# Decode attention on one core: keys and values streamed together in sets of four groups, with the softmax maximum

## The chip, the core and the metric

The kernel runs on one core of a Trainium2 chip. The metric is the device time of one execution in microseconds; the lower the better. A core has five engines that run side by side: PE (matrix multiply, with its weight loads shown as PEld), DVE (vector), ACT (activations), POOL and SP. Each works through its own list of instructions in order and waits on semaphores for the others. SP, ACT and POOL also issue transfers, which 16 DMA engines carry out.

## What is computed

The reference normalises x (8 rows of 512), and runs two branches on it: attention against cached keys and values, and a gated feed-forward network. Cut to what matters:

```python
xn = _layernorm(x)
q = (xn @ wq)                     # 8 rows, 32 heads of 128
k = k_cache[:, :, Sk - W:, :]     # W = 1024 of 4096 positions, 8 kv heads, 4 query heads each
v = v_cache[:, :, Sk - W:, :]
scores = einsum("bhqd,bhkd->bhqk", q, k) * 128 ** -0.5
p = softmax(scores)
s = einsum("bhqk,bhkd->bhqd", p, v) ... @ wo
g = silu((gelu(xn @ w_gate) * (xn @ w_up)) @ w_down)
return x + s * g
```

A pair of a kv head and a batch row is called a group here: 64 groups, each with 1,024 keys and 1,024 values of 128 bf16 numbers (256 KB each) and four query rows.

## The kernel before

It is written in tiles; a scheduler orders the instructions of each engine from their dependencies and allocates buffers, so the program's order is only a hint.

**Weights.** SP issues x (L74) and wq (L77, 4 MB in one transfer); ACT issues w_gate and w_down (L79, L83), POOL issues w_up (L81). The three queues share the 16 DMA engines.

**Head.** x is normalised (L90 to L99), transposed (L120), and multiplied by wq in 128 small products (L135) into q, kept transposed as `qT_all`. The feed-forward branch is two up-projections (L153), an activation chain between ACT and DVE (L163 to L177), the down-projection of 14 products with 512 columns (L181) and the gate `g_sb` (L189 to L193).

**Key stage.** For each group: a 256 KB load of keys (L203, six buffers), eight 128x128 transposes on PE into one PSUM bank (L211), a copy of the 1,024 columns to SBUF on DVE (L217), eight products of the transposed keys with the four query columns (L221), and an Exp on ACT (L228), without subtracting a maximum, into `pT_all`, which holds all 64 groups.

**Sums.** Four products with a matrix of ones, 512 columns each (L243), each reduced on DVE (L252), and one reciprocal of 256 columns (L258).

**Value stage.** For each group: a 256 KB load of values (L269, 20 buffers), eight products of four columns (L277) and a multiplication by the reciprocal (L284). After each kv head, 512 KB of wo are loaded (L292) and four products of 512 columns add that head's projection to `s_ps` (L300).

**End.** Two DVE instructions (L309, L311) and the store (L312).

Of the kernel before, what the change touches and what calls it, by code (L numbers as in the profile page):

```python
# [12 lines left out]
FP32 = mybir.dt.float32  # L13


@with_exitstack
def kernel(
# [12 lines left out]
):  # L30
    nc = tc.nc

# [7 lines left out]
    NDC = D // 128  # L40
    NFC = F // 128
    NSC = W // 128
    inv_sqrt_dh = float(Dh) ** -0.5

    P = nc.NUM_PARTITIONS
    NG = Hkv * B
    GB = 16
# [6 lines left out]
    kT_pool = ctx.enter_context(tc.tile_pool(name="kT_pool", bufs=4))  # L54
    v_pool = ctx.enter_context(tc.tile_pool(name="v_pool", bufs=20))
    small = ctx.enter_context(tc.tile_pool(name="small", bufs=3))
# [11 lines left out]
    )  # L68
    ones_pp = consts.tile([P, P], BF16, name="ones_pp")
    nc.vector.memset(ones_pp, 1.0)  # L70

    x_flat = A_x.flatten_outer_dims()
    x_sb = persist.tile([B, D], BF16, name="x_sb")
    nc.sync.dma_start(out=x_sb, in_=x_flat)  # L74

    wq_sb = weights.tile([P, NDC, Hq * Dh], BF16, name="wq_sb")
    nc.sync.dma_start(out=wq_sb, in_=A_wq.rearrange("(k p) n -> p k n", p=P))  # L77
    wg_sb = weights.tile([P, NDC, F], BF16, name="wg_sb")
    nc.scalar.dma_start(out=wg_sb, in_=B_w_gate.rearrange("(k p) n -> p k n", p=P))  # L79
    wu_sb = weights.tile([P, NDC, F], BF16, name="wu_sb")  # L80
    nc.gpsimd.dma_start(out=wu_sb, in_=B_w_up.rearrange("(k p) n -> p k n", p=P))  # L81
    wd_sb = weights.tile([P, NFC, D], BF16, name="wd_sb")
    nc.scalar.dma_start(out=wd_sb, in_=B_w_down.rearrange("(k p) n -> p k n", p=P))  # L83
    wo_sb = weights.tile([P, Hq, D], BF16, name="wo_sb")

    eps_sb = consts.tile([B, 1], FP32, name="eps_sb")
    nc.vector.memset(eps_sb, 1e-5)

# [17 lines left out]
    )  # L106

    xnT_sb = persist.tile([P, NDC, B], BF16, name="xnT_sb")
    qT_all = persist.tile([P, B, Hq], BF16, name="qT_all")
    oT_all = persist.tile([P, Hq, B], BF16, name="oT_all")  # L110
    hT_sb = persist.tile([P, NFC, B], BF16, name="hT_sb")
    g_sb = persist.tile([B, D], FP32, name="g_sb")
    pT_all = persist.tile([P, NG, NSC, rep], BF16, name="pT_all")
    sums_sb = persist.tile([P, NG, rep], FP32, name="sums_sb")
    recip_all = persist.tile([P, NG, rep], FP32, name="recip_all")

    with tc.tile_pool(name="ps_xnT", bufs=1, space=bass.MemoryType.PSUM) as ps_xnT_pool:
        xnT_ps = ps_xnT_pool.tile([P, NDC, B], BF16, name="xnT_ps")
        for k in range(NDC):
            nc.tensor.transpose(  # L120
                xnT_ps[:, k, :],
                xhat[:, k * 128 : (k + 1) * 128],
                ident[0:B, 0:B],
            )
        nc.vector.tensor_copy(out=xnT_sb, in_=xnT_ps)

    HB = 8
    qctx = ExitStack()
    ps_q = qctx.enter_context(tc.tile_pool(name="ps_q", bufs=2, space=bass.MemoryType.PSUM))
    for m0 in range(0, Hq, HB):  # L130
        qT_ps = ps_q.tile([P, HB, B], FP32, name="qT_ps")
        for mi in range(HB):
            m = m0 + mi
            for k in range(NDC):
                nc.tensor.matmul(  # L135
                    qT_ps[:, mi, :],
                    wq_sb[:, k, m * Dh : (m + 1) * Dh],
                    xnT_sb[:, k, :],
                    start=(k == 0),
                    stop=(k == NDC - 1),  # L140
                )
        nc.vector.tensor_copy(  # L142
            out=qT_all[:, :, m0 : m0 + HB],
            in_=qT_ps.rearrange("p h b -> p b h"),
        )

    fctx = ExitStack()
    ffn_ps = fctx.enter_context(tc.tile_pool(name="ffn_ps", bufs=1, space=bass.MemoryType.PSUM))
    gu_ps = ffn_ps.tile([P, NFC, 2, B], FP32, name="gu_ps")
    for j in range(NFC):  # L150
        for w, wsb in enumerate((wg_sb, wu_sb)):
            for k in range(NDC):
                nc.tensor.matmul(  # L153
                    gu_ps[:, j, w, :],
                    wsb[:, k, j * 128 : (j + 1) * 128],
                    xnT_sb[:, k, :],
                    start=(k == 0),
                    stop=(k == NDC - 1),
                )
    zT = gu_ps[:, :, 0, :]  # L160
    uT = gu_ps[:, :, 1, :]
    z2 = ffn_sb.tile([P, NFC, B], FP32, name="z2")
    nc.scalar.activation(out=z2, in_=zT, func=ACT.Square)  # L163
    nc.vector.tensor_scalar(
        out=z2, in0=z2, scalar1=0.044715, scalar2=1.0, op0=ALU.mult, op1=ALU.add
    )
    u3 = ffn_sb.tile([P, NFC, B], FP32, name="u3")
    nc.vector.tensor_tensor(out=u3, in0=z2, in1=zT, op=ALU.mult)
    th = ffn_sb.tile([P, NFC, B], FP32, name="th")
    nc.scalar.activation(out=th, in_=u3, func=ACT.Tanh, scale=0.7978845608028654)  # L170
    gm = ffn_sb.tile([P, NFC, B], FP32, name="gm")
    nc.vector.tensor_scalar(
        out=gm, in0=th, scalar1=0.5, scalar2=0.5, op0=ALU.mult, op1=ALU.add
    )
    gz = ffn_sb.tile([P, NFC, B], FP32, name="gz")
    nc.vector.tensor_tensor(out=gz, in0=gm, in1=zT, op=ALU.mult)
    nc.vector.tensor_tensor(out=hT_sb, in0=gz, in1=uT, op=ALU.mult)  # L177

    f_ps = ffn_ps.tile([B, D], FP32, name="f_ps")
    for j in range(NFC):  # L180
        nc.tensor.matmul(  # L181
            f_ps,
            hT_sb[:, j, :],
            wd_sb[:, j, :],
            start=(j == 0),
            stop=(j == NFC - 1),
        )
    th2 = ffn_sb.tile([B, D], FP32, name="th2")
    nc.scalar.activation(out=th2, in_=f_ps, func=ACT.Tanh, scale=0.5)  # L189
    nc.vector.tensor_scalar(  # L190
        out=th2, in0=th2, scalar1=0.5, scalar2=0.5, op0=ALU.mult, op1=ALU.add
    )
    nc.vector.tensor_tensor(out=g_sb, in0=th2, in1=f_ps, op=ALU.mult)  # L193

    p1ctx = ExitStack()
    ps_kT = p1ctx.enter_context(tc.tile_pool(name="ps_kT", bufs=2, space=bass.MemoryType.PSUM))
    ps_sc = p1ctx.enter_context(tc.tile_pool(name="ps_sc", bufs=2, space=bass.MemoryType.PSUM))

    gi = 0
    for hkv in range(Hkv):  # L200
        for b in range(B):
            k_sb = k_pool.tile([P, NSC, Dh], BF16, name="k_sb")
            nc.sync.dma_start(  # L203
                out=k_sb,
                in_=A_k_cache[b, hkv, win0:Sk, :].rearrange(
                    "(p c) d -> p c d", c=NSC
                ),
            )
            kT_ps = ps_kT.tile([P, W], BF16, name="kT_ps")
            for c in range(NSC):  # L210
                nc.tensor.transpose(  # L211
                    kT_ps[:, c * 128 : (c + 1) * 128],
                    k_sb[:, c, :],
                    ident,
                )
            kT = kT_pool.tile([P, W], BF16, name="kT")
            nc.vector.tensor_copy(out=kT, in_=kT_ps)  # L217
            sc_ps = ps_sc.tile([P, NSC, rep], FP32, name="sc_ps")
            qg = qT_all[:, b, hkv * rep : (hkv + 1) * rep]
            for c in range(NSC):  # L220
                nc.tensor.matmul(  # L221
                    sc_ps[:, c, :],
                    kT[:, c * 128 : (c + 1) * 128],
                    qg,
                    start=True,
                    stop=True,
                )
            nc.scalar.activation(  # L228
                out=pT_all[:, gi, :, :],
                in_=sc_ps,  # L230
                func=ACT.Exp,
                scale=inv_sqrt_dh,
            )
            gi += 1

    p1ctx.close()
    fctx.close()
    qctx.close()

    with tc.tile_pool(name="ps_sum", bufs=2, space=bass.MemoryType.PSUM) as ps_sum:  # L240
        for i in range(NG // GB):
            sums_ps = ps_sum.tile([P, GB * NSC * rep], FP32, name="sums_ps")
            nc.tensor.matmul(  # L243
                sums_ps,
                ones_pp,
                pT_all[:, i * GB : (i + 1) * GB, :, :].rearrange(
                    "p g c j -> p (g c j)"
                ),
                start=True,
                stop=True,  # L250
            )
            nc.vector.tensor_reduce(  # L252
                out=sums_sb[:, i * GB : (i + 1) * GB, :],
                in_=sums_ps.rearrange("p (g c j) -> p g j c", g=GB, c=NSC, j=rep),
                axis=AX.X,
# [87 lines left out]
```

## Time and profile before

| | |
|---|---|
| median of 3 runs | 150.63 us (149.76 to 152.62) |
| span of the profiled execution | 149.5 us |
| PE, PEld busy | 97.0 us (65%), 73.4 us (49%) |
| DVE, ACT busy | 64.2 us (43%), 16.5 us (11%) |
| moved by DMA | 47.74 MB, mean 319 GB/s |

The profiled execution is one run seen by the hardware profiler; its span goes from its first to its last instruction. The page gives busy time by engine; the span in 40 equal slices (busy tenths by engine, the clock granted to PE in tenths, DMA share and GB/s); DMA queues; the chain of work that ended last; and groups of instructions. A line of a group has the source line, engine, operation, output and inputs with their shapes, then the count, the busy time in us, the mean of one in ns, and the idle time of the engine just before them with what released it. Matmuls overlap one another, so their mean in ns is longer than the time that one of them holds PE; that time is the distance between starts in the timeline, whose columns are start, length, engine, line, operation, and count, with the idle time ahead in brackets. The table of stretches has busy time (and count of instructions) by engine, then the granted clock (1.00 is full), DMA share and GB/s.

### The profile page before, as it was taken

Reading aid. Unit: us, or ns where it says so; the run is one execution under the profiler, and the core shown is the slowest. Engines: PE = TensorE matmul, PEld = TensorE weight load, DVE = VectorE, ACT = ScalarE, POOL = GpSimd, SP = SyncE. Lnnn points to the kernel's source line nnn. Section 1 sums busy time; section 2 is a strip of 40 time slices with the busy share of each in tenths; the row PEclk is TensorE's granted clock in tenths of the full one; section 3 lists DMA queues with packets and bytes.
Section 4 is the critical chain, followed back from the end, with each engine's and each line's share of the span. In section 5 each row is a group of like instructions: output and inputs, shape, how many; then the busy total and the mean of one; then the engine's idle time right before and its main releaser. Section 6 shows DMA issues by size and latency. Waiting matters only on the chain.

```text
span 149.5 us, 4236 instructions
## 1 busy us (share of the span) xinstructions
PE 97.0 (65%) x1830; PEld 73.4 (49%) x1830; DVE 64.2 (43%) x154; ACT 16.5 (11%) x70; POOL 1.4 (1%) x6
## 2 busy tenths in 40 slices
PE   0000137499988896998998996597474748585760
PEld 0000127497466785987876874453433334342420
DVE  2100001057296885788788885831211121121213
ACT  4000000052122221222222221000000000000000
POOL 3000000000000000000000000000000000000000
PEclk9999999999999999689999999755555555555555
DMA  4999999957999699889989899999999999999900
GB/s 117 430 419 416 407 403 372 372 161 212 315 390 368 211 342 325 252 278 298 298 321 323 263 311 309 393 372 378 372 380 371 376 357 380 337 386 380 349 30 2
DMA packets 25843, 47.74 MB, mean 319 GB/s; under 512 B 2256, under 2 KB 8160, under 8 KB 25312
## 3 DMA queue, kind: packets, MB, share of 16 engines
q1 hardware_dynamic: 23216, 41.97, 79.9%
q10 hardware_dynamic: 2336, 3.67, 7.1%
q0 software_dynamic: 272, 1.84, 2.9%
q8 instruction: 14, 0.23, 0.6%
q14 instruction: 5, 0.04, 0.1%
HBM read 47.46 MB, written 0.01 MB: 318 GB/s over the span
## 4 chain that ended last, share of the span: by engine, by line
DMA 66%; PE 24%; DVE 5%; issue 3%; SPq 1%
DMA v_sb<-in_A_v_cache_dram 22%; DMA k_sb<-in_A_k_cache_dram 17%; DMA wq_sb<-in_A_wq_dram 15%; DMA wo_sb<-in_A_wo_dram 12%; PE kT_ps L211 10%; PE s_ps L300 4%; PE sc_ps L221 4%; DVE kT L217 3%; PE qT_ps L135 2%; PE f_ps L181 2%; PE gu_ps L153 1%; SPq L269 1%; DVE tmp L309 0%; DVE out_sb L311 0%; SPq L292 0%
## 5 line engine op out<-in xcount | busy, mean ns | idle before, releaser
L217 DVE COPY kT<-kT_ps 128x1024 bf16<-128x1024 bf16 x64 | 43.6, 690 | 14.4 <-PE kT_ps L211 14.1
L211 PE MATMUL kT_ps<-ident,k_sb 128*128 128x128 bf16 x512 | 41.6, 228 | 3.2 <-DMA k_sb<-in_A_k_cache_dram 3.2
L211 PEld LDWEIGHTS <-k_sb 128*128 128x128 bf16 x512 | 31.3, 102 | 3.8 <-DMA k_sb<-in_A_k_cache_dram 3.8
L284 DVE TENSOR_TENSOR oT_all<-oT_ps,recip_all 128x4 bf16<-128x4 f32 x64 | 11.0, 175 | 36.4 <-PE oT_ps L277 35.4
L277 PE MATMUL oT_ps<-pT_all,v_sb 128*128 128x4 bf16 x512 | 19.9, 167 | 10.2 <-DMA v_sb<-in_A_v_cache_dram 7.3
L277 PEld LDWEIGHTS <-v_sb 128*128 128x128 bf16 x512 | 16.8, 105 | 19.4 <-DMA v_sb<-in_A_v_cache_dram 10.6
L221 PE MATMUL sc_ps<-qT_all,kT 128*128 128x4 bf16 x512 | 22.7, 166 | 3.8 <-DVE kT L217 1.7
L221 PEld LDWEIGHTS <-kT 128*128 128x128 bf16 x512 | 17.9, 97 | 10.0 <-DVE kT L217 8.5
L300 PE MATMUL s_ps<-wo_sb,oT_all 128*8 128x512 bf16 x32 | 14.9, 620 | 8.0 <-DMA wo_sb<-in_A_wo_dram 8.0
L228 ACT ACTIVATE pT_all<-sc_ps 128x32 bf16<-128x32 f32 x64 | 12.6, 197 | 43.9 <-PE sc_ps L221 43.9
L153 PE MATMUL gu_ps<-xnT_sb,wg_sb 128*128 128x8 bf16 x56 | 3.4, 168 | 12.5 <-DMA wg_sb<-in_B_w_gate_dram 10.4
L142 DVE CAST qT_all<-qT_ps 128x64 bf16<-128x64 f32 x4 | 0.9, 225 | 21.3 <-PE qT_ps L135 21.3
L300 PEld LDWEIGHTS <-oT_all 128*8 128x8 bf16 x32 | 3.3, 106 | 12.8 <-issue 10.3
L153 PEld LDWEIGHTS <-wg_sb 128*128 128x128 bf16 x56 | 2.7, 104 | 10.5 <-DMA wg_sb<-in_B_w_gate_dram 10.5
L135 PE MATMUL qT_ps<-xnT_sb,wq_sb 128*128 128x8 bf16 x128 | 3.6, 168 | 3.4 <-DMA wq_sb<-in_A_wq_dram 3.4
L135 PEld LDWEIGHTS <-wq_sb 128*128 128x128 bf16 x128 | 3.5, 104 | 3.5 <-DMA wq_sb<-in_A_wq_dram 3.5
L153 PEld LDWEIGHTS <-wu_sb 128*128 128x128 bf16 x56 | 2.6, 104 | 5.2 <-DMA wu_sb<-in_B_w_up_dram 3.0
L153 PE MATMUL gu_ps<-xnT_sb,wu_sb 128*128 128x8 bf16 x56 | 3.1, 168 | 2.9 <-DMA wu_sb<-in_B_w_up_dram 2.9
L163 ACT ACTIVATE z_381<-gu_ps 128x112 f32<-128x112 f32 x1 | 0.3, 264 | 26.8 <-PE gu_ps L153 26.8
L252 DVE TENSOR_REDUCE sums_sb<-sums_ps 128x64 f32<-128x512 f32 x4 | 2.7, 684 | 1.1 <-PE sums_ps L243 1.1
L181 PE MATMUL f_ps<-wd_sb,hT_sb 128*8 128x512 bf16 x14 | 3.2, 379 | 0.0
L120 PE MATMUL xnT_ps<-ident,xhat 8*128 8x8 bf16 x4 | 0.3, 168 | 4.4 <-DVE xhat L99 4.4
(33 smaller groups left out, 15.9 us busy)
## 6 DMA issues: line engine op xcount, KB each, us to landing
k_sb<-in_A_k_cache_dram SPq DMA_DIRECT2D x64, 256.0 KB, 4.3
v_sb<-in_A_v_cache_dram SPq DMA_DIRECT2D x64, 256.0 KB, 6.1
wq_sb<-in_A_wq_dram SPq DMA_DIRECT2D x1, 4096.0 KB, 22.0
wo_sb<-in_A_wo_dram SPq DMA_DIRECT2D x8, 512.0 KB, 6.2
wg_sb<-in_B_w_gate_dram ACTq DMA_DIRECT2D x1, 1792.0 KB, 14.3
wd_sb<-in_B_w_down_dram ACTq DMA_DIRECT2D x1, 1792.0 KB, 32.1
wu_sb<-in_B_w_up_dram POOLq DMA_DIRECT2D x1, 1792.0 KB, 16.9
x_sb<-in_A_x_dram SPq DMA_DIRECT2D x1, 8.0 KB
```

What stands on the lines that cost most here:

```text
L135: nc.tensor.matmul(qT_ps[:, mi, :], wq_sb[:, k, m * Dh : (m + 1) * Dh], xnT_sb[:, k, :], start=(k == 0), stop=(k == NDC - 1),)
L153: nc.tensor.matmul(gu_ps[:, j, w, :], wsb[:, k, j * 128 : (j + 1) * 128], xnT_sb[:, k, :], start=(k == 0), stop=(k == NDC - 1),)
L181: nc.tensor.matmul(f_ps, hT_sb[:, j, :], wd_sb[:, j, :], start=(j == 0), stop=(j == NFC - 1),)
L211: nc.tensor.transpose(kT_ps[:, c * 128 : (c + 1) * 128], k_sb[:, c, :], ident,)
L217: nc.vector.tensor_copy(out=kT, in_=kT_ps)
L221: nc.tensor.matmul(sc_ps[:, c, :], kT[:, c * 128 : (c + 1) * 128], qg, start=True, stop=True,)
L228: nc.scalar.activation(out=pT_all[:, gi, :, :], in_=sc_ps, func=ACT.Exp, scale=inv_sqrt_dh,)
L252: nc.vector.tensor_reduce(out=sums_sb[:, i * GB : (i + 1) * GB, :], in_=sums_ps.rearrange("p (g c j) -> p g j c", g=GB, c=NSC, j=rep), axi ...
L269: nc.sync.dma_start(out=v_sb, in_=A_v_cache[b, hkv, win0:Sk, :].rearrange("(p c) d -> p c d", c=NSC),)
L277: nc.tensor.matmul(oT_ps, v_sb[:, c, :], pT_all[:, gi, c, :], start=(c == 0), stop=(c == NSC - 1),)
L284: nc.vector.tensor_tensor(out=oT_all[:, hkv * rep : (hkv + 1) * rep, b], in0=oT_ps, in1=recip_all[:, gi, :], op=ALU.mult,)
L300: nc.tensor.matmul(s_ps, oT_all[:, h, :], wo_sb[:, h, :], start=(h == 0), stop=(h == Hq - 1),)
```

## The change

The kernel is rewritten around one loop, and its order is now written by hand: `manual_schedule()` keeps the instructions of each engine in program order.

- All loads go through SP's queue, in the order x, wq (four transfers), keys of set 0, w_gate and w_up (two transfers each, alternating), keys of set 1, w_down (two), and then inside the loop. Keys and values are loaded two groups at a time (512 KB).
- A set is four groups. Step q of the loop issues the loads of keys of set q+2, values of set q and, every second step, 512 KB of wo; transposes and scores set q (one group of transposes ahead); finds the maximum of set q-1; and works on the values of set q-2. There are 16 sets and 18 steps. The up-projections stand at step 1, the down-projection at step 3, and the projection of a kv head at every second step from step 4, the last one behind the loop.
- The softmax now subtracts a maximum. `max_keys` reduces the scores of a set over the eight key blocks on DVE and transposes the result on PE in fp32. `max_all` reduces over the partitions, negated, scales an identity of 16 with it, and adds it to the scores in PSUM by eight fp32 products with ones; then one Exp for the set.
- The sums are eight products of 16 columns for each set, with a reciprocal of 16 columns; one multiplication normalises a set.
- The eight PSUM banks are held throughout: one shared by q, the feed-forward products and the projection, two for transposed keys, two for scores, one each for the maximum, the sums and the values.

The core of the diff (lines removed are those of the stages above, quoted with the kernel):

```diff
+    ctx.enter_context(tc.manual_schedule())
...
+    QG = 4
+    PG = 2
+    NG = Hkv * B
+    NQ = NG // QG
+    QC = QG * rep
+    SH = B // QG
+    LAG = 2
...
-    v_pool = ctx.enter_context(tc.tile_pool(name="v_pool", bufs=20))
+    kT_pool = ctx.enter_context(tc.tile_pool(name="kT_pool", bufs=3))
+    v_pool = ctx.enter_context(tc.tile_pool(name="v_pool", bufs=8))
...
+    def load_k(pair):
+        hkv, b = divmod(pair * PG, B)
+        t = k_pool.tile([P, PG, NSC * Dh], BF16, name="k_sb")
+        nc.sync.dma_start(
+            out=t,
+            in_=A_k_cache[b : b + PG, hkv, win0:Sk, :].rearrange(
+                "g (p c) d -> p g (c d)", c=NSC
+            ),
+        )
+        return t
...
+    def transposes(g):
+        kT_ps = ps_kT.tile([P, W], BF16, name="kT_ps")
+        src = k_sb[g // PG]
+        for c in range(NSC):
             nc.tensor.transpose(
+                kT_ps[:, c * P : (c + 1) * P],
+                src[:, g % PG, c * Dh : (c + 1) * Dh],
+                ident,
+            )
+        kT[g] = kT_pool.tile([P, W], BF16, name="kT")
+        nc.vector.tensor_copy(out=kT[g], in_=kT_ps)
...
+    def scores(g):
+        q, i = divmod(g, QG)
+        hkv, b = divmod(g, B)
+        if i == 0:
+            sc[q] = ps_sc.tile([P, QG, NSC, rep], FP32, name="sc_ps")
+        for c in range(NSC):
+            nc.tensor.matmul(
+                sc[q][:, i, c, :],
+                kT[g][:, c * P : (c + 1) * P],
+                qT_all[:, b, hkv * rep : (hkv + 1) * rep],
+                start=(i == 0 and c == 0),
+                stop=False,
+                skip_group_check=True,
+            )
+
+    def max_keys(q):
+        mx = small.tile([P, QG, rep], FP32, name="mx")
+        nc.vector.tensor_reduce(
+            out=mx, in_=sc[q].rearrange("p g c j -> p g j c"), axis=AX.X, op=ALU.max
+        )
+        mxT[q] = ps_mx.tile([QC, P], FP32, name="mxT_ps")
+        nc.tensor.transpose(mxT[q], mx.rearrange("p g j -> p (g j)"), ident_f)
+
+    def max_all(q):
+        nm = small.tile([QC, 1], FP32, name="nm")
+        nc.vector.tensor_reduce(
+            out=nm, in_=mxT[q], axis=AX.X, op=ALU.max, negate=True
+        )
+        dm = small.tile([QC, QG, rep], FP32, name="dm")
+        nc.vector.tensor_scalar(
+            out=dm.rearrange("p g j -> p (g j)"),
+            in0=ident_f[0:QC, 0:QC],
+            scalar1=nm[:, 0:1],
+            scalar2=None,
+            op0=ALU.mult,
+        )
+        for c in range(NSC):
+            nc.tensor.matmul(
+                sc[q][:, :, c, :],
+                ones_f,
+                dm,
+                start=False,
+                stop=(c == NSC - 1),
+                skip_group_check=True,
+            )
+        pT[q] = p_pool.tile([P, QG, NSC, rep], BF16, name="pT")
+        nc.scalar.activation(out=pT[q], in_=sc[q], func=ACT.Exp, scale=inv_sqrt_dh)
...
+    transposes(0)
+    gu_ps = None
+    for q in range(NQ + LAG):
+        if q + 2 < NQ:
+            load_k_set(q + 2)
+        if q < NQ:
+            load_v_set(q)
+        if q < NQ and q % SH == SH - 1:
+            load_wo(q // SH)
+        if q == 1:
+            gu_ps = ffn_up()
+            ffn_act(gu_ps)
+        if q == 3:
+            ffn_down()
+        v = q - LAG
+        if v >= 0:
+            sums(v)
+            if v % SH == 0 and v > 0:
+                project(v // SH - 1)
+        for i in range(QG):
+            g = q * QG + i
+            if g + 1 < NG:
+                transposes(g + 1)
+            if i == 0 and 1 <= q <= NQ:
+                max_keys(q - 1)
+            if g < NG:
+                scores(g)
+            if i == 2 and 1 <= q <= NQ:
+                max_all(q - 1)
+            if v >= 0:
+                values(v * QG + i)
+        if v >= 0:
+            normalise(v)
```

`values` is eight products of four columns for a group, `sums` eight products of 16 columns with ones and the reciprocal, `normalise` one multiplication for a set, and `project` four products of 512 columns.

## The prediction

> **What bounds the kernel now.** I read the page first (busy rows, slices, groups), then the chain of waits, then the timeline of a few groups, then the table of stretches cut where the granted clock changes. The slices show two stages; see where PE and DVE run high with DMA uneven, and where DMA stays at nine while PEclk falls.
>
> ```profile
> PE   0000137499988896998998996597474748585760
> ...
> DVE  2100001057296885788788885831211121121213
> ...
> PEclk9999999999999999689999999755555555555555
> DMA  4999999957999699889989899999999999999900
> GB/s 117 430 419 416 407 403 372 372 161 212 315 390 368 211 342 325 252 278 298 298 321 323 263 311 309 393 372 378 372 380 371 376 357 380 337 386 380 349 30 2
> ```
>
> Up to 30 us weights arrive; to about 92 us keys are transposed and scored (40 to 86 us moves 304 GB/s: PE and DVE, with six key buffers, pace it); then values stream at 370 GB/s and only the transfers pace it, at half clock, which there costs nothing. The groups give the price of each operation:
>
> ```profile
> L217 DVE COPY kT<-kT_ps 128x1024 bf16<-128x1024 bf16 x64 | 43.6, 690 | 14.4 <-PE kT_ps L211 14.1
> L284 DVE TENSOR_TENSOR oT_all<-oT_ps,recip_all 128x4 bf16<-128x4 f32 x64 | 11.0, 175 | 36.4 <-PE oT_ps L277 35.4
> L300 PE MATMUL s_ps<-wo_sb,oT_all 128*8 128x512 bf16 x32 | 14.9, 620 | 8.0 <-DMA wo_sb<-in_A_wo_dram 8.0
> L252 DVE TENSOR_REDUCE sums_sb<-sums_ps 128x64 f32<-128x512 f32 x4 | 2.7, 684 | 1.1 <-PE sums_ps L243 1.1
> ```
>
> The timeline has how long PE is held by a burst of eight (start to next start), and when the copy begins. At full clock:
>
> ```profile
> 69.33 0.61 PE L211 MATMUL kT_ps<-ident,k_sb 128*128 128x128 bf16 x8
> 69.78 0.34 PE L221 MATMUL sc_ps<-qT_all,kT 128*128 128x4 bf16 x8
> 69.98 1.34 DVE L217 COPY kT<-kT_ps 128x1024 bf16<-128x1024 bf16 x2 [0.27 <-PE kT_ps L211]
> 69.98 0.61 PE L211 MATMUL kT_ps<-ident,k_sb 128*128 128x128 bf16 x8
> ```
>
> At half clock:
>
> ```profile
> 62.91 1.01 PE L211 MATMUL kT_ps<-ident,k_sb 128*128 128x128 bf16 x8
> 63.71 0.40 PE L221 MATMUL sc_ps<-qT_all,kT 128*128 128x4 bf16 x8
> 63.96 0.69 DVE L217 COPY kT<-kT_ps 128x1024 bf16<-128x1024 bf16 x1 [0.38 <-PE kT_ps L211]
> 63.97 0.27 PE L211 MATMUL kT_ps<-ident,k_sb 128*128 128x128 bf16 x1
> ```
>
> So eight transposes (T) hold PE 0.45 us at full and 0.81 at half clock, eight scores (S) 0.20 and 0.26 (eight value products, V, the same: 24 in 0.74 at 93.90); the copy starts 0.65 or 1.05 us after T does. The stretches, each 3.41 us between possible changes of the clock (the second runs from a fall to the return):
>
> ```profile
> core 0: us, PE busy (x) PEld busy (x), PEclk, DMA share, GB/s
> 57.83:61.24 3.41, 1.57 (x23) 1.18 (x22) 1.00 0.80 267
> 61.24:64.65 3.41, 3.25 (x30) 2.52 (x28) 0.50 0.87 264
> 88.55:91.96 3.41, 1.85 (x24) 1.35 (x24) 1.00 0.94 275
> 102.20:105.61 3.41, 0.00 (x0) 0.00 (x0) 0.50 1.05 379
> ```
>
> These count transposes alone; all matmuls there are 47, 54, 56 and 44. In moving columns (128 a transpose, 4 a score, 512 each for the four projections of the last): 3,040, after which the clock fell; 3,936 at half, after which it rose; 3,200, held; 2,208 at half, not raised.
>
> **The change, part by part.** One step is a set of four groups; 16 sets, two more steps to drain. Each engine keeps the order written.
>
> Transfers: the bytes stay (47.74 MB). One set moves 2.1 MB plus 0.26 of wo: 6.4 us at 370. K is issued two sets ahead and V two sets before use, so loads are early unless a step is shorter than that. SP's issues go from 139 to 84 at 0.33 to 0.43 us, all hidden; wg, wd (ACT queue) and wu (POOL queue) now stand behind wq in SP's queue, so wq no longer shares its 22 us with them, and they come later (head, below). A V load that waits for its buffer holds back the K loads queued behind it; its buffers are four sets deep, so this costs nothing unless loads set the pace. Pairs of 512 KB instead of 256 keep 2 KB per partition; I give them nothing, since 256 KB already run at 370.
>
> One step on PE, full clock (half clock in brackets), is the sum:
> - sums 0.21 (0.26). Its reciprocal of 16 columns, 0.15 to 0.3 by L97 and L258, is hidden behind T.
> - T of the next group, its copy, then the new reduction over key blocks (128 elements: between L284's 0.175 and L252's 0.684, by elements 0.30), then the transpose of that maximum. It stands behind the copy on DVE and ahead of S on PE: 0.65+0.69+0.30+0.05 = 1.69 (2.09) before it can start. PE idles some 1.2 us.
> - fp32 transpose of 16x128: no row; 0.06 (two bf16 transposes) to 0.45 (eight); 0.30, nearer the upper as operands are double width.
> - S, V, T, S, V: 1.27 (1.85).
> - T of the third group, copy, second reduction 0.30, scaled identity 0.15 (L97), 0.08 of gaps, then the eight products that add minus the maximum: 0.65+0.69+0.30+0.15+0.08 = 1.87 (2.27). S runs inside; PE idles 1.1 us again.
> - these eight fp32 products: no row; 0.20 (eight S) to 3.4 (eight 512-column products at 0.43). By columns, 16, they are nearest to S; twice the bytes in weights and in data: 4 x 0.20 = 0.80.
> - V, T, S, V: 1.07 (1.59).
> Sum 7.21 us (9.16), above the 6.4 of the transfers and above DVE's own 2.76+0.30+0.30+0.15+0.25+0.19 = 3.95. Nothing is below zero: all of it is added work between two dependent engines, in written order. Behind each of PE's two waits stand S, V and the next T, and behind T the copies of DVE; nothing else is ready for PE there, so both are paid in full.
>
> Hidden, with its cover: Exp of 128 columns instead of 32 (0.197 now, some 0.3) is needed one step later; the normalising, now 16 of 16 columns instead of 64 (11.0 us of DVE), ends 0.2 to 0.6 us into the next step, ahead of the first V that needs its bank; without that cover each costs its own length a step, 5 us in all. The four large sums, their reductions (2.7) and the reciprocal of 256 columns (1.75), some 3 us of wait at 92 to 95.6, go, and were hidden by value transfers already under way.
>
> The Trainium skill, FP8 and Floating Point Precision, TensorE Precision Notes, has a true fp32 product make four passes through the array; by that the eight would be an estimate of 0.8 from S, and no run here shows it.
>
> The clock. A full-clock step has 32x128 + 64x4 + 8x16 + 256 = 4,736 moving columns, 2,240 in 3.41 us (2,600 if fp32 counts four times). 3,040 lost the clock. At half, 4,736 per 9.16 us is 1,763 (2,050), and 2,208 didn't raise it. So the stream falls to half and stays; only the stretches with a projection (+2,048) may rise, six times, worth some 3 us in all. The Trainium skill, TensorE: Matmul & The Clock Gate, Why this matters for your kernels, asks only for no PE idle gap above about 3 us; by it, with gaps of 1.2, the clock would hold. The trace disagrees: the stretch at 57.83 has no gap above 1.14 us and ends in a fall.
>
> Head: wq is 4.2 MB, with 0.97 MB moved by 5 us (so a start at 2.7) and 418 GB/s after: landed at 13. PE then does q (3.58 us, 128 products) and set 0, but the fourth step needs K of set 1, queued behind wg and wu: 10 MB, 26.4 to 27. Then S, up-projection (112 x 27 ns = 3.0), and the activation chain 31.2 to 33.85 (Square 0.26, two DVE 0.49, table load 1.28, Tanh 0.30, three DVE 0.73). DVE runs in order, so the next copy waits for it: the first maximum's transpose is at 34.9. The rest of step 1, without V: 4.5 (5.8), to 39.4 (40.7). Step 2 to 46.6 (49.9). Step 3 adds 14 products of 512 columns, 3.0 (6.0; 5.0 as dense work raises the clock), and 0.9 for DVE behind the gate: 57.7 (64.9).
> Steps 4 to 15: 12 steps, 86.5 (109.9), plus six projections, four products 0.86 (1.72) with a wait for the last normalising of 0.5 (0.4): 8.2 (12.8), less 3 for rises. To 152.4 (184.6). Two draining steps: 3.8+2.7 (4.7+3.7). Tail as now, from the last projection's end (145.66) to 149.5: 3.8.
>
> ```profile
> 143.76 1.87 PE L300 MATMUL s_ps<-wo_sb,oT_all 128*8 128x512 bf16 x4 [0.96 <-DMA wo_sb<-in_A_wo_dram]
> 145.66 0.68 DVE L309 TENSOR_TENSOR tmp<-s_ps,g_sb 8x512 f32<-8x512 f32 x1 [2.65 <-PE s_ps L300]
> ```
>
> Span 162.7 (196.8). The median of 150.63 is 1.1 above the profiled span of 149.5, so 164 (198). Removed and worth nothing by itself: the separate key and value stages, now overlapped, since PE, not the transfers, sets the step.
>
> **Rivals.**
> 1. The clock holds: 164; 152 with the lower fp32 prices, 202 with the upper. For it: columns count only as I infer, and 3,040 against 3,200 is a thin edge. Against: 2,240 is well below both. Chance 0.20, of which 0.05 lie within 2% of now.
> 2. Faster: the maximum's two chains hide, because DVE is free at the moment they are needed. Full-clock PE work is then 7.21 - 2.46 = 4.75 and transfers decide: 2.7 + 7.9 MB at 418 (18.8) + 39.6 MB at 370 (107) + 5.8 (wo landing to end now) + 1.1 = 135. It decides from a step below 6.3 us, where 12 and two half-filled steps give back the 13 us between 164 and 151. Against: copy, reduction and transpose are each written in that order. Chance 0.07. The Trainium skill, DMA: Bandwidth & Descriptors, Bandwidth, would have larger transfers give more of the peak; that too helps only here, and 256 KB at 370 says little is left.
> 3. The fp32 products cost their upper end: half clock 198 + 14 x 2.7 = 236. Chance 0.05 at or near that end.
>
> **How the numbers follow.** Half clock as summed: 0.68; its own range is 186 (lower fp32 ends: 14 x 0.84 off) to 222 (about two thirds of the way up). That is the forecast, 198. The range 152 to 222 takes in the full-clock rival, leaving out the faster one and what is above, with the edge of "same": some 0.18. About 2% is what this measurement can tell from no change. Faster 0.07, same 0.05, slower 0.88.
>
> **What would show it.** Right: PEclk at 0.5 for most of the stream; two PE gaps of about 1.2 us in each step, released by the new reduction and by the scaled identity; a step of 9.2 us; DMA share well below full, loads landed long before use. Wrong: PEclk 1.0 (then 164), fp32 groups longer than 0.1 us a product, PE waiting for k_sb or v_sb (then transfers decide and 135 is near), or a wait of DVE or SP that I haven't named.

## The result and the profile after

The changed kernel takes 238.2 us (median of 4 runs, 236.55 to 239.49), against 150.5 before: 1.589 times as long, 95% interval 1.572 to 1.606. Runs more than 1.5% above the fastest run of their kernel are left out of the ratios here. The profiled execution has a span of 234.8 us. The forecast was slower, 198 us, in a range of 152 to 222; the direction holds and the time lies above the range.

Three rows of the 40 slices after, 5.9 us each:

```profile
PEclk9999999999965555575555555555555555555555
DMA  5999999998261575358543937275705944100000
GB/s 211 427 400 405 378 363 385 377 386 299 89 240 38 184 262 217 141 170 281 181 178 92 345 113 261 89 253 197 266 27 209 379 106 117 65 3 0 3 0 1
```

Before, DMA stood at eight or nine almost throughout. Now it does so only up to some 56 us, while the weights and the first sets of keys and values land; after that it is full for a stretch and then nearly idle, about 160 GB/s on average from 100 to 222 us. Next to nothing is moved in the last 29 us. The clock of PE is half after 65.8 us, but for one stretch of 3.4 us from 99.9.

The nines at the start of the PEclk row have to be read with care. Eight transposes, ahead of the down-projection and behind it, after (start, us, engine, line, operation):

```profile
54.33 1.01 PE L272 MATMUL kT_ps<-ident,k_sb 128*128 128x128 bf16 x8
60.60 0.61 PE L272 MATMUL kT_ps<-ident,k_sb 128*128 128x128 bf16 x8
```

The first has the length of a half-clock burst, the second that of a full-clock one. So PE ran at half up to some 59 us as well, and at full only from there to 65.8: where the trace has no clock record yet, the row shows a nine. This holds for every kernel here; the kernel before ran at half until 33.9 us.

Who paces the loads is in the waits of SP's queue, after (total us, times, longest):

```profile
SPq L92 <- PE kT_ps L272: 112.1, 23, 9.9
```

Loads of keys wait 112 us for PE to have transposed the keys that sit in their buffer. The costliest groups after (line, engine, operation, count, then busy us, mean ns of one, and idle before it with its releaser):

```profile
L278 DVE COPY kT<-kT_ps 128x1024 bf16<-128x1024 bf16 x64 | 44.2, 690 | 130.1 <-PE kT_ps L272 130.1
L317 PE MATMUL sc_ps<-dm,ones_f 16*128 16x16 f32 x256 | 57.4, 370 | 15.5 <-DVE dm L309 15.5
L272 PE MATMUL kT_ps<-ident,k_sb 128*128 128x128 bf16 x512 | 62.9, 302 | 6.8 <-DMA k_sb<-in_A_k_cache_dram 6.8
L317 PEld LDWEIGHTS sc_ps<-dm,ones_f 16*128 16x128 f32 x256 | 55.7, 325 | 16.9 <-DVE dm L309 16.9
```

The copy is as long as before, one by one, and now waits 130 us for PE. New at the top are the fp32 products that add the negated maximum: 16 x 8 products are 256 records, two weight loads and two matmuls for each product, and the loads alone are busy 55.7 us. The 130 us and the 112 us are not losses of their own: they say that DVE and the loads wait for PE.

One step in order, from its first copy, at half clock (start, us, engine, line, operation; the idle time in brackets):

```profile
110.48 0.69 DVE L278 COPY kT<-kT_ps 128x1024 bf16<-128x1024 bf16 x1 [0.56 <-PE kT_ps L272]
111.09 0.28 DVE L297 TENSOR_REDUCE mx<-sc_ps 128x16 f32<-128x128 f32 x1
111.42 0.38 PE L301 MATMUL mxT_ps<-ident_f,mx 128*16 128x128 f32 x1 [0.98 <-DVE mx L297]
...
113.35 1.01 PE L272 MATMUL kT_ps<-ident,k_sb 128*128 128x128 bf16 x8
...
114.40 0.69 DVE L278 COPY kT<-kT_ps 128x1024 bf16<-128x1024 bf16 x1 [0.59 <-PE kT_ps L272]
115.01 0.27 DVE L305 TENSOR_REDUCE nm<-mxT_ps 16x1 f32<-16x128 f32 x1
115.31 0.22 DVE L309 TENSOR_SCALAR dm<-ident_f,nm 16x16 f32<-16x16 f32 x1
...
115.59 3.59 PE L317 MATMUL sc_ps<-dm,ones_f 16*128 16x16 f32 x16 [1.03 <-DVE dm L309]
119.11 0.37 PE L349 MATMUL o_ps<-pT,v_sb 128*128 128x4 bf16 x8
```

Both PE waits are there, 0.98 and 1.03 us, the first released by a reduction and the second by the scaled identity that follows one; each reduction stands behind a copy. The fp32 products hold PE from 115.59 to 119.11. From the sums of this step (109.22) to those of the next (120.62) are 11.4 us; a step with a projection takes 13.7 (from 115.59 to 129.25, product to product).

### The profile page after: what moved, and what is told of

It is laid out like the page before. It is cut to its first block, busy times and chain, and to the rows that moved or that the text cites. A ratio compares the mean times of both kernels' runs of the same rounds, so it can differ in the third digit from the quotient of the medians.

```text
span 234.8 us, 4836 instructions
## 1 busy us (share of the span) xinstructions
PE 176.2 (75%) x2226; PEld 152.8 (65%) x2226; DVE 64.6 (28%) x164; ACT 8.4 (4%) x22; POOL 0.5 (0%) x5
## 4 chain that ended last, share of the span: by engine, by line
PE 68%; DVE 17%; DMA 7%; SPq 5%; issue 2%; ACT 1%
PE sc_ps L317 24%; PE kT_ps L272 21%; DVE kT L278 11%; DMA k_sb<-in_A_k_cache_dram 7%; PE s_ps L374 6%; PE o_ps L349 6%; PE sc_ps L286 3%; PE mxT_ps L301 2%; PE f_ps L251 2%; SPq L128 2%; DVE dm L309 2%; DVE nm L305 1%; DVE mx L297 1%; PE gu_ps L219 1%; SPq L132 1%
## 5 line engine op out<-in xcount | busy, mean ns | idle before, releaser
L317 PE MATMUL sc_ps<-dm,ones_f 16*128 16x16 f32 x256 | 57.4, 370 | 15.5 <-DVE dm L309 15.5
L272 PE MATMUL kT_ps<-ident,k_sb 128*128 128x128 bf16 x512 | 62.9, 302 | 6.8 <-DMA k_sb<-in_A_k_cache_dram 6.8
L317 PEld LDWEIGHTS sc_ps<-dm,ones_f 16*128 16x128 f32 x256 | 55.7, 325 | 16.9 <-DVE dm L309 16.9
L272 PEld LDWEIGHTS <-k_sb 128*128 128x128 bf16 x512 | 47.8, 136 | 12.0 <-DMA k_sb<-in_A_k_cache_dram 6.9
L286 PEld LDWEIGHTS <-kT 128*128 128x128 bf16 x512 | 25.8, 113 | 1.2 <-DVE kT L278 0.2
L349 PE MATMUL o_ps<-pT,v_sb 128*128 128x4 bf16 x512 | 22.1, 167 | 0.1
L301 PE MATMUL mxT_ps<-ident_f,mx 128*16 128x128 f32 x16 | 5.9, 369 | 17.5 <-DVE mx L297 17.5
L326 ACT ACTIVATE pT<-sc_ps 128x128 bf16<-128x128 f32 x16 | 4.4, 278 | 182.1 <-PE sc_ps L317 182.1
L331 PE MATMUL sums_ps<-pT,ones_pp 128*128 128x16 bf16 x128 | 5.8, 174 | 0.0
L331 PEld LDWEIGHTS <-ones_pp 128*128 128x128 bf16 x128 | 4.7, 104 | 0.4 <-issue 0.4
```

The source lines that it names most:

```text
L272: nc.tensor.transpose(kT_ps[:, c * P : (c + 1) * P], src[:, g % PG, c * Dh : (c + 1) * Dh], ident,)
L286: nc.tensor.matmul(sc[q][:, i, c, :], kT[g][:, c * P : (c + 1) * P], qT_all[:, b, hkv * rep : (hkv + 1) * rep], start=(i == 0 and c == 0), ...
L301: nc.tensor.transpose(mxT[q], mx.rearrange("p g j -> p (g j)"), ident_f)
L317: nc.tensor.matmul(sc[q][:, :, c, :], ones_f, dm, start=False, stop=(c == NSC - 1), skip_group_check=True,)
L331: nc.tensor.matmul(sums_ps, ones_pp, pT[q][:, :, c, :], start=(c == 0), stop=(c == NSC - 1),)
L349: nc.tensor.matmul(o_ps[q][:, i, :], src[:, g % PG, c * Dh : (c + 1) * Dh], pT[q][:, i, c, :], start=(c == 0), stop=(c == NSC - 1),)
```

## The experiments

The theory tested: a step is what PE runs and waits for in the written order, and its parts add up: fp32 products 3.5 us, two waits 1.0 each, the rest stretched by the half clock. The rivals: the transfers in one queue pace the kernel; the clock alone is the loss; a removed wait only uncovers another. Each kernel is one run beside a run of the kernel before (151.4 to 152.4 us) unless a number of runs is given.

**The maximum taken out.**

```diff
...      # also gone: both reductions, the fp32 transpose, the scaled identity, the eight products
     def max_all(q):
...
         pT[q] = p_pool.tile([P, QG, NSC, rep], BF16, name="pT")
         nc.scalar.activation(out=pT[q], in_=sc[q], func=ACT.Exp, scale=inv_sqrt_dh)
...
-            if i == 0 and 1 <= q <= NQ:
-                max_keys(q - 1)
```

> This kernel leaves the maximum out (no reductions over it, no fp32 transpose, no fp32 products; Exp stands at the same place), as the kernel before does. Chain theory (a step is what PE runs and waits for in written order): of the 11.4 us step at half clock, the eight fp32 products take 3.6, their wait 1.1, the wait for the transposed maximum 1.1 and the transpose 0.2 to 0.4; 5.4 to 5.5 remain, 1.1 more on average for projections, about 6.5, where the transfers (6.4 a set at 370 GB/s) come in: 135 to 145 us. Transfer theory (large transfers in one queue, with their buffer waits, set the pace): the step stays above 9 us, over 190 us. Clock theory (half clock is most of the loss): the step loses the products but the stream stays at half clock, above 160 us.

It took 137.5 us. Slices, and the chain that ended last, of this kernel:

```profile
PEclk9999999999999995999995599959955995555555
DMA  3999999999999999999999999999999999999400
...
DMA 52%; PE 28%; SPq 9%; DVE 6%; ACT 2%; issue 1%
```

DMA is full from the second slice to the end of the loads, and the chain is now transfers. The clock still falls in many stretches, and it costs little, since DMA stays full all the same. So the loads in one queue, in pairs and in sets, are not what made the change slow; with the same loads and no maximum the kernel beats the one before. The clock rival forecast more than 160 us, but this run doesn't settle it: without the maximum the clock is full for about half of the time from 40 us on, so two things changed at once. The run with bf16 products, below, settles it.

**One fp32 product in place of eight.**

```diff
-        dm = small.tile([QC, QG, rep], FP32, name="dm")
+        dm = small.tile([QC, QG, NSC, rep], FP32, name="dm")
...
-            in0=ident_f[0:QC, 0:QC],
+            in0=ident_w,
...
-        for c in range(NSC):
-            nc.tensor.matmul(
-                sc[q][:, :, c, :],
...
+        nc.tensor.matmul(
+            sc[q].rearrange("p g c j -> p (g c j)"),
+            ones_f,
+            dm.rearrange("p g c j -> p (g c j)"),
```

> The eight fp32 products of 16 columns become one of 128 columns, with the identity repeated eight times beforehand; result and columns moved are the same. If an fp32 product costs per weight load (two loads of 0.22 us each): 16 loads become 2, 3.6 us becomes about 0.5, 16 x 3.1 = 50 us less, some 188 us. If it costs per column moved: no change, 236 to 240 us.

It took 190.9 us, 47 less, with the columns unchanged. The product in this kernel:

```profile
109.22 0.79 PE L322 MATMUL sc_ps<-dm,ones_f 16*128 16x128 f32 x2 [0.99 <-DVE dm L315]
```

Two records hold PE for 0.72 us (the next instruction starts at 109.94) instead of sixteen for 3.52. The cost goes with the number of products, each with its two weight loads, and not with the columns. That the loads are the larger part is read from the changed kernel: from 115.59 to 119.11 PEld is busy for 3.48 of the 3.52 us.

**Eight bf16 products.**

```diff
-        dm = small.tile([QC, QG, rep], FP32, name="dm")
+        dm = small.tile([QC, QG, rep], BF16, name="dm")
...
-                ones_f,
+                ones_pp[0:QC, :],
```

> The eight products take bf16 operands (ones and the scaled identity; the constant subtracted is the same for all keys of a query, so its rounding drops out of the softmax). If fp32 operands are the cost: 3.6 us becomes 0.22 to 0.30 as for eight sums, 16 x 3.3 = 53 us less, about 185 us. If the wait for the accumulation bank or the 16-row operand is the cost: 230 us or more.

It took 183.6 us, 55 less. The group in this kernel:

```profile
L317 PE MATMUL sc_ps<-dm,ones_pp 16*128 16x16 bf16 x128 | 5.7, 169 | 15.4 <-DVE dm L309 15.4
...
106.08 0.36 PE L317 MATMUL sc_ps<-dm,ones_pp 16*128 16x16 bf16 x8 [1.03 <-DVE dm L309]
106.37 0.37 PE L349 MATMUL o_ps<-pT,v_sb 128*128 128x4 bf16 x8
```

The same bank, the same 16 rows and the same wait (15.4 us in total, 15.5 in the changed kernel), but 128 records and 0.29 us a set. What was dear was the fp32 operand. The clock is no better here than in the changed kernel (0.52 on average from 67 to 180 us) and 55 us are gone: the half clock alone was not the loss.

**The reductions ahead of the copies.** The products stay in fp32; only the order changes. (The comments are added here and say what each function now holds.)

```diff
+            if i == 0 and 1 <= q <= NQ:
+                max_keys(q - 1)      # reduction alone
+            if i == 2 and 1 <= q <= NQ:
+                max_all(q - 1)       # reduction and scaled identity alone
             if g + 1 < NG:
                 transposes(g + 1)
             if i == 0 and 1 <= q <= NQ:
-                max_keys(q - 1)
+                max_turn(q - 1)      # fp32 transpose
             if g < NG:
                 scores(g)
             if i == 2 and 1 <= q <= NQ:
-                max_all(q - 1)
+                max_add(q - 1)       # fp32 products, Exp
```

> Order alone: the first reduction is written ahead of the transposes of the step, and the second reduction and scaled identity ahead of the transposes of the third group, so that DVE does them before the two copies. Chain theory: the two PE waits (17.5 and 15.5 us in total, 1.0 to 1.1 us each) shrink to 0.1 to 0.4: 25 to 33 us less, 205 to 213 us. If these waits only take the place of another wait behind them: 235 us or more.

It took 192.6 us, 46 less, where 25 to 33 were expected. The waits went as forecast: for the transposed maximum from 17.5 to 3.5 us in total, for the scaled identity from 15.5 to 0.2. That is 29 us. The rest, some 16 us, is put down to the clock, which no run tests alone: once it has fallen for the first time, it is raised in six stretches of 3.4 us instead of one, and five more such stretches can give back 17 us at most. The fp32 products at full clock, in this kernel:

```profile
125.30 1.86 PEld L326 LDWEIGHTS sc_ps<-dm,ones_f 16*128 16x128 f32 x16 [0.18 <-DVE dm L314]
125.31 1.95 PE L326 MATMUL sc_ps<-dm,ones_f 16*128 16x16 f32 x16
```

Sixteen loads in 1.86 us, some 0.11 each, against 0.22 at half clock: these loads follow the clock, so a set whose products fall into a full-clock stretch saves 1.7 us here.

**Both edits together, with one fp32 product.**

> Both edits of the two runs before: one fp32 product of 128 columns, and the reductions written ahead of the copies. Chain theory: of the 11.4 us step at half clock 3.1 and about 2.2 go, 6.1 remain and 1.1 for projections, close to the 6.4 of the transfers; with the clock back part of the time, 140 to 158 us. If the 46 us of the order run were only the clock coming back, and not the waits, the two gains would overlap: above 165 us.

It took 137.0 us: 101 us less than the changed kernel, about the sum of the two gains (47 and 46), and at the floor of the transfers (379 GB/s from 40 to 124 us). No other wait of PE took the place of those removed; the transfers set the pace now.

**Both edits together, with bf16 products, timed.**

> The maximum kept, with bf16 products and the reductions written ahead of the copies. Chain theory: step 5.9 us at half clock and 1.1 for projections, less where the clock is up; the transfers' 6.4 us decide most steps: 137 to 150 us, faster than the kernel before. Otherwise, if another wait takes the place of those removed: above 155 us.

It took 138.1 us (median of 4 runs, 137.3 to 141.2), ratio to the kernel before 0.915, interval 0.908 to 0.923. So the maximum itself can be had for about a microsecond (137.2 without it, next run); this kernel computes it and beats the one before.

**The kernel without the maximum, timed, and the same with 256 KB loads.** The edit of the second, against the first:

```diff
-    PG = 2
+    PG = 1
...
-    k_pool = ctx.enter_context(tc.tile_pool(name="k_pool", bufs=6))
+    k_pool = ctx.enter_context(tc.tile_pool(name="k_pool", bufs=12))
-    v_pool = ctx.enter_context(tc.tile_pool(name="v_pool", bufs=8))
+    v_pool = ctx.enter_context(tc.tile_pool(name="v_pool", bufs=16))
```

> The kernel without the maximum again, timed: 136 to 139 us; its DMA share is full from 10 to 125 us, so the transfers bound it.

> Without the maximum, and loads of keys and values of 256 KB (one group) instead of 512 KB, with twice the buffers: same bytes, 64 issues more on SP at 0.33 to 0.43 us. If the larger transfers are worth nothing, as forecast: within 2 us of the run beside it. If size matters: the set's 2.1 MB at a lower rate, 4 us or more slower.

137.2 us with 512 KB (4 runs, ratio 0.910, interval 0.902 to 0.917) and 137.0 with 256 KB (4 runs, 0.910, 0.903 to 0.918): no difference. The stretch from 40 to 124 us, with 512 KB loads:

```profile
40.00:124.00 84.00, 71.47 (x1423) 59.61 (x1421) 40.84 (x81) 4.08 (x14) 0.00 (x0) 0.78 1.05 380
```

and with 256 KB loads:

```profile
40.00:124.00 84.00, 76.09 (x1437) 64.08 (x1433) 41.19 (x84) 4.35 (x15) 0.00 (x0) 0.71 1.05 376
```

The last two numbers are DMA share and GB/s. The gain over the kernel before goes with keeping that rate throughout, where its key stage moved 304; it does not come from the size.

**Useless work to hold the clock.** Added to the kernel with bf16 products (183.6 us), in both places where PE waits (`fill` is called ahead of the fp32 transpose and ahead of the eight products):

```diff
+    def fill(pool, name):
+        t = pool.tile([P, 512], FP32, name=name)
+        for _ in range(3):
+            nc.tensor.matmul(t, ident, wq_sb[:, 0, 0:512], start=True, stop=True)
```

> The kernel with bf16 products, order as in the changed kernel, plus useless work: three bf16 products of 512 columns in each of the two places of a step where PE waits for the maximum (nothing reads them). Clock theory (moving columns in a stretch of 3.41 us decide the clock): the step goes from about 4,740 to 7,810 columns; once the down-projection has raised the clock, 7,810 in 6.6 us is about 4,000 in 3.41 us, above the 3,200 to 3,300 that held it; six products take 1.3 us at full clock, inside 2.1 us of waits: 150 to 160 us, faster than the same kernel without them (183.6). If the clock doesn't matter or isn't held: 184 to 195 us.

It took 156.3 us: 96 products more and 27 us less. PEclk in this kernel:

```profile
PEclk9999999999999999999999999999999999999975
```

Here too the first nines are half clock by the length of the transposes. The trace has the clock raised at 39.4 us, ahead of the down-projection that was expected to raise it, and held until 148.6.

**The same with one product in each place.**

> The same with one product in each place: 5,760 columns in a step, about 2,400 in 3.41 us at half clock and 3,000 at full, too few to hold it. Clock theory: little gained, 170 to 185 us. If idle gaps alone decide the clock (this shortens each gap by as much as a third), it would be held: 150 to 160 us.

It took 188.4 us, 5 more than without, and a miss of the expectation by 3. Why it is slower is not shown; at half clock each of these products holds PE for 0.43 us, and the clock was full for 7 us in all, against 17 in the kernel without them. PEclk in this kernel:

```profile
PEclk9999999999999555555555555555555555555555
```

By the trace the clock is full from 53.6 to 60.4 us alone. So one product for each wait doesn't hold it, and three do. This pair doesn't tell columns from gaps, since three products also leave shorter gaps than one. What tells them apart is a stretch of the kernel with the reductions ahead of the copies, and the one behind it (us, busy by engine, then clock, DMA share and GB/s):

```profile
96.90:100.32 3.41, 3.41 (x65) 3.37 (x64) 1.22 (x3) 0.28 (x1) 0.00 (x0) 1.00 0.98 337
100.32:103.73 3.41, 3.09 (x22) 1.48 (x20) 0.74 (x5) 0.00 (x0) 0.00 (x0) 0.50 0.90 288
```

In the first, by the profile, PE is busy from end to end, with sixteen fp32 records in it and so only some 1,900 columns, and the clock falls all the same. Gaps alone don't decide it. (The trace lacks 30 of the 32 matmul records of the added products here, and 30 of the 96 in the kernel with three; their number is read from their weight loads.)

**The scheduler's order in place of the written one.**

```diff
-    ctx.enter_context(tc.manual_schedule())
```

> The changed kernel without the line that keeps the written order: the scheduler orders each engine. Chain theory: the 57 us of fp32 products stay, the two waits (33 us) may be filled: 195 to 235 us. If the written order alone were the loss: below 160 us.

It took 213.3 us, 25 less than with the written order and far above 160. The order costs something, and a scheduler gets part of it back; the products remain.

## Why the prediction was wrong, point by point

**The step that failed: the eight fp32 products, put at 0.80 us.** They take 3.52 us at half clock. Sixteen sets times 2.72 us is 43.5 us; the forecast span of 196.8 with that term corrected is 240.3, and the measured span is 234.8. Taking the term out again bears this out: one product in place of eight gave 47 us, bf16 products 55. I chose the price by moving columns, 16, the nearest to the scores, and doubled for the width of both operands. But these products are paced by their weight loads, and I had no row for an fp32 load of 128 columns: it takes 0.22 us at half clock and 0.11 at full, where a bf16 load with its product takes 0.03, and an fp32 product takes two. The sum also had 0.80 at both clocks, where its bf16 bursts grow at half clock. The sign named for being wrong, more than 0.1 us a product, came: 0.44.

The upper end of the price, 3.4, and the third rival, 236 us, came within a few us, by luck. The 3.4 was the price of 512 moving columns, which these products don't have, and the rival counted it for 14 sets where 16 run (242 by its own working), while the rest of the sum was some 5 us too long. The range failed with the term: it stopped two thirds of the way up to that end.

On this the Trainium skill, TensorE: Matmul & The Clock Gate, LDWEIGHTS and Weight-path perf modes, says that a load takes its columns divided by 1.2, in ns, and that the fast weight load is not used for fp32. For 128 columns that is an estimate of 107 ns. The full-clock 0.11 us agrees; that it doubles at half clock is measured here and not in that formula. The Trainium skill, FP8 and Floating Point Precision, TensorE Precision Notes, has four passes for an fp32 product, by which the estimate was the same 0.8. The trace shows two pairs of load and matmul for each product, at 0.44 us the two at half clock, so the estimate doesn't hold for these products.

**The two waits of PE: right.** Forecast 1.2 and 1.1 us a step, measured 0.98 and 1.03 as the profile counts them, released by the instructions named. Removing them gave at least what they cost (order run), and no other wait of PE came in their place.

**The clock: right, and the columns hold up as a rough measure.** Half for the stream, as forecast; of six projections that might raise it, one did. With three filling products the stretches of 3.41 us had about 3,400 columns or more, through gaps, and kept the clock; with one, 2,850 lost it. The edge itself is not settled: in the changed kernel the stretch from 96.48 to 99.90, with 3,228 columns at half clock, raised it, and the one from 144.27 to 147.68, with 3,296, did not, so plain columns are not the whole measure.

The Trainium skill, TensorE: Matmul & The Clock Gate, Why this matters for your kernels, asks for no idle gap above about 3 us. After 60 us no gap in the kernel with one filling product is longer than about 1.1 us, and the clock was at half all the same; the measurement decides.

**The transfers: right.** Hidden in the changed kernel, loads early and waiting for buffers; the floor of 135 us of the second rival, worked out from rows, is close to the 137 to 138 us of the four kernels without the long chain. The larger transfers were given nothing and are worth nothing.

**The rest of the sum: close.** Forecast step at half clock with the products corrected 9.16 + 2.72 = 11.88, measured 11.4; the fp32 transpose takes 0.18 us instead of 0.30, a burst of value products 0.21 instead of 0.26. A projection adds 2.25 us to a step (forecast 2.12). The first transposed maximum starts at 35.85 (forecast 34.9), the tail is 3.8 us, as forecast. Two terms of the full-clock sum, 1.27 and 1.07, come to 1.25 and 1.05 from their own bursts; the half-clock sum, which the forecast used, is not touched.

## What to carry to other kernels

Price a small matmul by its weight load as well as by its columns, and where no row shows the load for that type, forecast with the upper bound at least half believed: here one unpriced load was worth 44 us. A reduction that PE waits for should be written ahead of a long copy on the same engine; moving two of them gave 46 us, waits and clock together. Read the clock at the start of a trace from the length of a known burst, not from the PEclk row. When PE waits often, ask whether it moves enough columns to keep its clock (here stretches of 3.4 us with 2,850 and 3,040 lost it, and one with 3,200 kept it), before counting on the durations of a full-clock stage.

## What the runs showed of the hardware

- An fp32 product with 128 weight columns is two records, each 0.22 us at half clock and 0.11 at full, with 16 moving columns; with 128 moving columns the two hold PE for 0.72 us at half clock.
- Work that nobody needs can shorten a kernel: 96 products of 512 columns took it from 183.6 to 156.3 us, with PE at full clock from 39.4 to 148.6 us.
- PE can lose its clock while it is busy from end to end: a stretch of 3.41 us with sixteen fp32 records and some 1,900 moving columns ended in a fall, at 100.32 us of the kernel with the reductions ahead.
- PE starts at half clock in every trace here (transposes 0.107 us apart, 0.056 at full), though the PEclk row shows nines until the first record.
- Keys and values in 512 KB or 256 KB transfers from one queue move at 380 and 376 GB/s.
